# Two steps of the second phase's weight split on GpSimd, and a later place for w_k's load and split

## The chip, the cores and the metric

The kernel runs on one core of one Trainium2 chip. The metric is device time in microseconds (us), smaller is better; a time given for a kernel is the median of its runs. The engines are named as in the profile: PE is TensorE (PEld its weight loads), DVE VectorE, ACT ScalarE, POOL GpSimd, SP the queue that issues the DMAs.

## What is computed

Three stages in a row, in float32: an attention between the tokens and a small state, a gated convolution layer ("first phase" of the kernel, with the attention), and a channel mix ("second phase"). Cut to what matters:

```python
# x: (8, 8, 512, 64)  state: (8, 8, 32, 64)
a = softmax(scale * x @ state.T);  xread = a @ state          # 512 rows a head
a2 = softmax(scale * state @ x.T); sread = a2 @ x             # 32 rows a head
x1 = concat([xread, sread])            # (8, 544, 512), heads side by side

h = relu(x1 @ w_in)                    # 512 -> 1024
c = conv over 3 neighbouring tokens of h, one weight per channel and tap
x2 = (h * sigmoid(c)) @ w_out          # 1024 -> 512

xk = mu_k * x2 + (1 - mu_k) * prev(x2);  xr = mu_r * x2 + (1 - mu_r) * prev(x2)
k = relu(xk @ w_k);  v = (k * k) @ w_v;  r = sigmoid(xr @ w_r)
out = r * v                            # (8, 544, 512)
```

The weights come as float64. The kernel splits each into a high and a low float32r part, and every product of two matrices is three TensorE products: high by high, high by low, low by high.

## The kernel before

**Phases and slots.** The work is written as a row of slots. In the first phase a slot is (1, t, f): batch t (0 to 7; t = 8 holds the 32 state rows of all batches) and f, one of eight blocks of 128 of the 1024 columns. In the second it is (2, t, f), t a piece of 384 or 512 tokens. A first-phase slot has five steps: g1_main (TensorE: the block's products, lines 423 to 444), g1_a (ScalarE relu into hb, L452, ScalarE's first tap into cacc, L468, VectorE's two other taps, L470; GpSimd sets hb's two border columns, L451, and copies its last columns to carry, L453), g1_b (sigmoid on ScalarE, L478, product with hb on VectorE, L479), g1_c (the gate's high part on ScalarE, L485, its low part on VectorE, L487, or on GpSimd for t up to 2), and g1_sec (TensorE: the gate's parts by w_out into four sums acc). For t = 8 GpSimd fills hb from carry (L456, L457). The text calls the gate of slot (1, t, f) simply (t, f). The second-phase steps are g2_main to g2_sec (L566 to 618); load_y (L525) and mix (L546) prepare its input.

**m.** For the batches after the first, attention's scores and w_in are first folded to a small matrix m per batch. pair_m (L229) makes it for two batches at a time, and each of its pieces leaves through four DMAs on SP (L248) into me0, me1 (even batch) and m_odd (odd batch). g1_main of the two batches reads those.

**The weights.** Weights.load (L131) issues the DMAs of a pair of blocks; Weights.split (L145) makes the two parts of a pair, 128 x 1024 columns at a time, in seven steps: L161 and L163 on ScalarE (the lower and the upper word of the float64), L164 on VectorE (sign), L165 on VectorE (the lower word's magnitude, clamped to a range), L166 on VectorE (joined), L168 on ScalarE (the high part), L169 on VectorE (the low part). The staging tiles raw and mid have two buffers each, which pair_m's pieces use too. In the second phase there are ten such pairs: four of w_k (tiles k0, k2, k4, k6), four of w_v (v0 twice, v4 twice), two of w_r (r0, r2). They are laid out from slot (1, 7, 2) on (L753 to 767), when the pool of attention's tiles is closed.

**What sets the order.** Each engine runs its own queue in order. The queues are made when the program is built, by a scheduler that takes instructions by a priority and by its own picture of when an operand is ready. A step's priority is 1000 times its slot number plus STAGE; weights get 500 times the half-slot in which they are needed, less 1000 (weight_at, L725). behind(i) (L174) adds an edge: what is written inside it stands behind instruction i on i's own engine.

Of the kernel before, what the change touches and what calls it, by code (L numbers as in the profile page):

```python
# [8 lines left out]
F32 = mybir.dt.float32  # L9
# [23 lines left out]
def tile_kernel(  # L33
# [38 lines left out]
    N = 512  # L72
# [47 lines left out]
    class Weights:  # L120

        def __init__(self, src, many, n, pool, tag="", home=None):
            self.src, self.many, self.n, self.pool, self.tag, self.home = src, many, n, pool, tag, home
            self.wide = src[0].dtype != F32
# [18 lines left out]
        def split(self, w, first=0):  # L145
# [6 lines left out]
            if not self.wide:  # L152
# [11 lines left out]
            nc.vector.scalar_tensor_tensor(v, e, 0x80000000, v, op0=ALU.bitwise_and, op1=ALU.bitwise_or)  # L164
            nc.vector.tensor_scalar(xf, xf, scalar1=2.0, scalar2=most, op0=ALU.max, op1=ALU.min)  # L165
            nc.vector.scalar_tensor_tensor(v, x, 3, v, op0=ALU.logical_shift_left, op1=ALU.bitwise_or)  # L166
            return (
                nc.scalar.activation(hi, vf, AF.Copy),  # L168
                nc.vector.tensor_tensor(lo, vf, hi.bitcast(F32), op=ALU.subtract),  # L169
            )  # L170
# [6 lines left out]

    def weight(src, key, tag, pool, k, many, group, home=None):


        r = Weights([src[k + i] for i in range(many)], many, N, stg, home=home)

# [46 lines left out]
    def pair_m(b, q, g):  # L229
# [16 lines left out]
        for j, rj in HALF:  # L246
            for i, ri in HALF:
                nc.sync.dma_start(out=m_of(b + j, q)[ri, :, g].bitcast(F32), in_=r[rj, :, i].bitcast(F32))  # L248

# [224 lines left out]
    def g1_b(t, f):  # L474
        n = width(t)
        s = st1[t, f]
        g = s["g"] = cp.tile([P, N], F32, tag="g", name="g")
        nc.scalar.activation(g[:, :n], s["a"][:, :n], AF.Sigmoid)  # L478
        nc.vector.tensor_tensor(g[:, :n], g[:, :n], s["hb"][:, 1:1 + n], op=ALU.mult)  # L479

# [269 lines left out]
    for i in range(len(slots) + 2):  # L750
        if i < len(slots):
            ph, t, f = slots[i]
            if (ph, t, f) == (1, B - 1, 2):  # L753
                ap_cm.__exit__(None, None, None)
                p2 = ctx.enter_context(tc.tile_pool(name="p2", bufs=1))
                for k in range(0, KF, 2):
                    w = weight(w_k, "k", "wk", p2, k, 2, 2)
                    h = h2 + 2 * k
                    weight_at(w, h, h - 4)
                for k in range(0, KF, 2):  # L760
                    w = weight(w_v, "v", "wa", wp, k, 2, 4)
                    h = h2 + 2 * k + 4
                    weight_at(w, h + 1, h - 3)
                for k in range(0, KC, 2):
                    w = weight(w_r, "r", "wb", wp, k, 2, 2)
                    h = h2 + 8
# [84 lines left out]
```

## Time and profile before

| | us |
|---|---|
| median of 3 runs | 886.2 |
| lowest, highest | 883.36, 887.11 |
| profiled execution | 881.77 |
| its span, first to last instruction | 879.9 |
| busy in it: PE, DVE, ACT, POOL | 853.5, 546.4, 545.6, 105.4 |

The profile is of one execution; its times run from the span's start. PE's busy time is 97% of the span, so what is read from the profile is where PE is not busy, or not at full clock, and which engine it waits for there. Busy shares of the other engines are means over phases that differ: VectorE is busy for 95% and more of many stretches of the first phase, and for about half of the second.

### The profile page before, as it was taken

How to read it: one execution, taken by the hardware profiler on the slowest of the kernel's cores; microseconds unless marked ns; L12 is line 12 of the kernel's file. 1: busy time of each engine (PE TensorE's matmuls, PEld its weight loads, DVE VectorE, ACT ScalarE, POOL GpSimd, SP SyncE). 2: the span in 40 equal slices, each digit the busy share in tenths (PEclk: the TensorE clock that was granted, in tenths of full speed). 3: DMA queues.
4: the chain of work that ended last, by engine and by line, in shares of the span. 5: the costliest groups of instructions: out<-in, count | busy, mean ns of one | idle time of the engine just before them, and what ended most of it. 6: DMA issues, size and time to landing. Idle time of an engine off the chain costs nothing.

```text
span 879.9 us, 11844 instructions
## 1 busy us (share of the span) xinstructions
PE 853.5 (97%) x4406; PEld 686.2 (78%) x4406; DVE 546.4 (62%) x908; ACT 545.6 (62%) x952; POOL 105.4 (12%) x215
## 2 busy tenths in 40 slices
PE   5989999999999997999999999999999999999997
PEld 2557787788778775899888888888888888888886
DVE  6899987899799879999645533425334253332311
ACT  6787875787578658888756645636356364553421
POOL 1144543422111111210000000000000000000000
PEclk7899999999999998999999999999999999999999
DMA  9351254525534364233210211011100111001010
GB/s 340 116 197 49 102 143 128 150 75 160 156 114 121 96 197 151 96 144 120 98 48 37 49 48 31 17 48 49 48 23 26 49 48 48 19 18 48 1 48 36
DMA packets 45512, 76.85 MB, mean 87 GB/s; under 512 B 8336, under 2 KB 30352, under 8 KB 43408
## 3 DMA queue, kind: packets, MB, share of 16 engines
q1 hardware_dynamic: 45456, 76.12, 26.6%
q8 instruction: 34, 0.56, 0.3%
q14 instruction: 22, 0.18, 0.1%
HBM read 45.66 MB, written 17.86 MB: 72 GB/s over the span
## 4 chain that ended last, share of the span: by engine, by line
PE 88%; DVE 5%; ACT 3%; DMA 2%; SPq 1%; issue 1%; DVEq 0%; ACTq 0%
PE acc L115 14%; PE acc L116 14%; PE acc L117 14%; PE kps L115 7%; PE kps L116 7%; PE kps L117 7%; PE rps L117 4%; PE rps L116 4%; PE rps L115 4%; PE hps L115 3%; PE hps L117 3%; PE hps L116 3%; PE p_s L297 2%; PE p_m L116 1%; PE p_m L117 1%; SPq L248 1%
## 5 line engine op out<-in xcount | busy, mean ns | idle before, releaser
L594 DVE TENSOR_TENSOR ks<-k,ks 128x512 fp32r<-128x512 f32 (+1 forms) x72 | 47.6, 662 | 119.8 <-ACT ks L593 119.2
L116 PE MATMUL kps<-xk,k 128*128 128x512 f32 (+1 forms) x288 | 110.1, 382 | 0.0
L115 PE MATMUL kps<-xk,k 128*128 128x512 f32 (+1 forms) x288 | 110.1, 383 | 0.0
L117 PE MATMUL kps<-xk,k 128*128 128x512 f32 (+1 forms) x288 | 110.0, 382 | 0.0
L116 PE MATMUL acc<-gs,out 128*128 128x512 f32 (+1 forms) x288 | 109.6, 382 | 0.0
L117 PE MATMUL acc<-gs,out 128*128 128x512 f32 (+1 forms) x288 | 109.1, 380 | 0.0
L115 PE MATMUL acc<-v,ks 128*128 128x512 f32 x272 | 106.7, 392 | 0.0
L116 PE MATMUL acc<-v,ks 128*128 128x512 f32 x272 | 105.9, 389 | 0.0
L117 PE MATMUL acc<-v,ks 128*128 128x512 f32 x272 | 105.8, 392 | 0.0
L470 DVE SCALAR_TENSOR_TENSOR cacc<-hb,vcol,cacc 128x512 f32<-128x512 f32 (+1 forms) x138 | 103.3, 759 | 3.2 <-ACT cacc L468 2.7
L115 PE MATMUL acc<-gs,out 128*128 128x512 f32 (+1 forms) x288 | 95.0, 391 | 5.8 <-ACT gs L485 5.8
L559 DVE SCALAR_TENSOR_TENSOR mix<-yt,muc,mix 128x384 f32<-128x384 f32 (+7 forms) x128 | 61.4, 500 | 47.0 <-ACT mix L557 46.2
L593 ACT ACTIVATE ks<-k 128x512 fp32r<-128x512 f32 (+1 forms) x72 | 43.5, 605 | 71.2 <-PE acc L117 71.0
L557 ACT ACTIVATE mix<-yt,om 128x384 f32<-128x384 f32 (+7 forms) x128 | 61.5, 516 | 33.0 <-DMA yt<-y 16.2
L580 ACT ACTIVATE k<-kps 128x512 f32<-128x512 f32 (+1 forms) x72 | 40.9, 569 | 50.4 <-PE kps L117 50.0
L115 PEld LDWEIGHTS acc<-gs,out 128*128 128x128 f32 x288 | 54.0, 192 | 18.3 <-ACT gs L485 7.3
L116 PEld LDWEIGHTS acc<-gs,out 128*128 128x128 f32 x288 | 54.2, 188 | 13.1 <-issue 2.5
L565 DVE TENSOR_TENSOR xr<-mix,xr 128x512 fp32r<-128x512 f32 (+1 forms) x36 | 23.8, 661 | 62.8 <-ACT xr L564 62.8
L117 PEld LDWEIGHTS acc<-gs,out 128*128 128x128 f32 x288 | 54.2, 188 | 10.6 <-issue 0.8
L116 PEld LDWEIGHTS kps<-xk,k 128*128 128x128 f32 x288 | 54.4, 189 | 10.4
L117 PEld LDWEIGHTS kps<-xk,k 128*128 128x128 f32 x288 | 54.3, 188 | 10.2
L115 PEld LDWEIGHTS kps<-xk,k 128*128 128x128 f32 x288 | 54.2, 188 | 10.2
(138 smaller groups left out, 1762.1 us busy)
## 6 DMA issues: line engine op xcount, KB each, us to landing
out<-r SPq DMA_DIRECT2D x34, 256.0 KB, 2.0
xT<-x_t SPq DMA_DIRECT2D x32, 256.0 KB, 4.0
xn<-x_n SPq DMA_DIRECT2D x8, 1024.0 KB, 4.9
y<-yo SPq DMA_DIRECT2D x8, 1024.0 KB, 4.3
me<-m SPq DMA_DIRECT2D x48, 128.0 KB, 2.4
m_odd<-m SPq DMA_DIRECT2D x48, 128.0 KB, 2.4
raw<-w_out SPq DMA_DIRECT2D x8, 512.0 KB, 4.7
raw<-w_k SPq DMA_DIRECT2D x8, 512.0 KB, 4.5
```

Source lines behind the costliest of these rows:

```text
L115: nc.tensor.matmul(ps, lh, rh, start=start and k == 0, stop=False)
L116: nc.tensor.matmul(ps, lh, rl, start=False, stop=False)
L117: nc.tensor.matmul(ps, ll, rh, start=False, stop=stop and k == last)
L248: nc.sync.dma_start(out=m_of(b + j, q)[ri, :, g].bitcast(F32), in_=r[rj, :, i].bitcast(F32))
L297: nc.tensor.matmul(self.v["s", g][NS * j:NS * (j + 1), :], sT[self.b][r, h // 2, h % 2], xT[self.b][r, h // 2], start=True, stop=True,)
L470: nc.vector.scalar_tensor_tensor(a[:, :n], hb[:, k:k + n], w[k], a[:, :n], op0=ALU.mult, op1=ALU.add)
L557: nc.scalar.activation(tmp[:, o:o + m], y[:, c, q - 1:q - 1 + m], AF.Copy, scale=om[:, i:i + 1])
L559: nc.vector.scalar_tensor_tensor(tmp[:, o:o + m], y[:, c, q:q + m], muc[:, i:i + 1], tmp[:, o:o + m], op0=ALU.mult, op1=ALU.add,)
L565: nc.vector.tensor_tensor(dst[t][:, 1, c, :n], tmp[:, :n], hi.bitcast(F32), op=ALU.subtract)
L580: nc.scalar.activation(k[:, :n], s["p"][:, :n], AF.Relu)
L593: nc.scalar.activation(ks[:, 0, :n], s["k2"][:, :n], AF.Copy)
L594: nc.vector.tensor_tensor(ks[:, 1, :n], s["k2"][:, :n], ks[:, 0, :n].bitcast(F32), op=ALU.subtract)
```

## The change

Two things. Weights takes a helper engine: for the second phase's weights that is GpSimd, which now does the clamp (L165) and the low part (L169); VectorE keeps L164 and L166. And w_k's load and split get fixed places: the load stands behind the last copy of m on SP, the split's ScalarE steps behind the sigmoid and its VectorE steps behind the gate product of slot (7, 0), that is batch 7's first gate.

```diff
--- before.py
+++ after.py
@@ -121,7 +121,8 @@
 
 
 
-        def __init__(self, src, many, n, pool, tag="", home=None):
+        def __init__(self, src, many, n, pool, tag="", home=None, helper=None):
+            self.helper = helper or nc.vector
             self.src, self.many, self.n, self.pool, self.tag, self.home = src, many, n, pool, tag, home
             self.wide = src[0].dtype != F32
 
@@ -162,11 +163,11 @@
             most = float.fromhex("0x1.dffffep+32")
             nc.scalar.activation(v, v, AF.Copy, scale=0.936 * 2.0**-29)
             nc.vector.scalar_tensor_tensor(v, e, 0x80000000, v, op0=ALU.bitwise_and, op1=ALU.bitwise_or)
-            nc.vector.tensor_scalar(xf, xf, scalar1=2.0, scalar2=most, op0=ALU.max, op1=ALU.min)
+            self.helper.tensor_scalar(xf, xf, scalar1=2.0, scalar2=most, op0=ALU.max, op1=ALU.min)
             nc.vector.scalar_tensor_tensor(v, x, 3, v, op0=ALU.logical_shift_left, op1=ALU.bitwise_or)
             return (
                 nc.scalar.activation(hi, vf, AF.Copy),
-                nc.vector.tensor_tensor(lo, vf, hi.bitcast(F32), op=ALU.subtract),
+                self.helper.tensor_tensor(lo, vf, hi.bitcast(F32), op=ALU.subtract),
             )
 
     W = {}
@@ -175,10 +176,23 @@
 
         return tc.issue_after(i.ins)
 
-    def weight(src, key, tag, pool, k, many, group, home=None):
-
-
-        r = Weights([src[k + i] for i in range(many)], many, N, stg, home=home)
+    marks = {}
+
+    def after(fn, *keys):
+
+
+        def run():
+            with ExitStack() as stack:
+                for key in keys:
+                    stack.enter_context(behind(marks[key]))
+                fn()
+
+        return run
+
+    def weight(src, key, tag, pool, k, many, group, **how):
+
+
+        r = Weights([src[k + i] for i in range(many)], many, N, stg, **how)
 
         def split(first=0, n=many):
             g = (key, "group", k // group)
@@ -245,7 +259,9 @@
         nc.vector.tensor_tensor(r[:, 1], src, r[:, 0].bitcast(F32), op=ALU.subtract)
         for j, rj in HALF:
             for i, ri in HALF:
-                nc.sync.dma_start(out=m_of(b + j, q)[ri, :, g].bitcast(F32), in_=r[rj, :, i].bitcast(F32))
+                marks["m"] = nc.sync.dma_start(
+                    out=m_of(b + j, q)[ri, :, g].bitcast(F32), in_=r[rj, :, i].bitcast(F32)
+                )
 
     class Attention:
         def __init__(self, b, ap):
@@ -475,8 +491,8 @@
         n = width(t)
         s = st1[t, f]
         g = s["g"] = cp.tile([P, N], F32, tag="g", name="g")
-        nc.scalar.activation(g[:, :n], s["a"][:, :n], AF.Sigmoid)
-        nc.vector.tensor_tensor(g[:, :n], g[:, :n], s["hb"][:, 1:1 + n], op=ALU.mult)
+        marks["sigmoid", t, f] = nc.scalar.activation(g[:, :n], s["a"][:, :n], AF.Sigmoid)
+        marks["gate", t, f] = nc.vector.tensor_tensor(g[:, :n], g[:, :n], s["hb"][:, 1:1 + n], op=ALU.mult)
 
     def g1_c(t, f):
         n = width(t)
@@ -754,15 +770,16 @@
                 ap_cm.__exit__(None, None, None)
                 p2 = ctx.enter_context(tc.tile_pool(name="p2", bufs=1))
                 for k in range(0, KF, 2):
-                    w = weight(w_k, "k", "wk", p2, k, 2, 2)
+                    w = weight(w_k, "k", "wk", p2, k, 2, 2, helper=nc.gpsimd)
+                    w = after(w[0], "m"), after(w[1], ("sigmoid", B - 1, 0), ("gate", B - 1, 0))
                     h = h2 + 2 * k
                     weight_at(w, h, h - 4)
                 for k in range(0, KF, 2):
-                    w = weight(w_v, "v", "wa", wp, k, 2, 4)
+                    w = weight(w_v, "v", "wa", wp, k, 2, 4, helper=nc.gpsimd)
                     h = h2 + 2 * k + 4
                     weight_at(w, h + 1, h - 3)
                 for k in range(0, KC, 2):
-                    w = weight(w_r, "r", "wb", wp, k, 2, 2)
+                    w = weight(w_r, "r", "wb", wp, k, 2, 2, helper=nc.gpsimd)
                     h = h2 + 8
                     weight_at(w, h, h - 2)
                 at_half(2 * i + 4, lambda: load_y(0, p2))
```

What the scheduler makes of it, at three places. The names carry buffer numbers here, to tell like rows apart; before and after number lines differently (L161 to L169 are L162 to L170 after, L452 is L468, L468 is L484, L478 is L494, L485 is L501, L487 is L503, L456 is L472).

First, ScalarE ahead of the high part of gate (6,4), which is gs_3355; hb_3361 is the relu of (6,6), g_3321 and g_3358 the sigmoids of (6,4) and (6,5). Before:

```order
L452 ACTIVATE hb_3361<-hps_3348 128x512
L168 ACTIVATE k0_4040<-raw_4037 128x1024
L478 ACT_TABLE_LOAD
L478 ACTIVATE g_3321<-cacc_3259 128x512
L478 ACTIVATE g_3358<-cacc_3328 128x512
L468 ACTIVATE cacc_3365<-hb_3361,vcol_97 128x512
L161 ACTIVATE mid_4135<-raw_4131 128x1024
L163 ACTIVATE raw_4131<-raw_4131 128x1024
L485 ACTIVATE gs_3355<-g_3321 128x512
```

and after, from the first tap of (6,5) on:

```order
L484 ACTIVATE cacc_3328<-hb_3324,vcol_97 128x512
L494 ACT_TABLE_LOAD
L494 ACTIVATE g_3321<-cacc_3259 128x512
L468 ACTIVATE hb_3361<-hps_3348 128x512
L494 ACTIVATE g_3358<-cacc_3328 128x512
L484 ACTIVATE cacc_3365<-hb_3361,vcol_97 128x512
L501 ACTIVATE gs_3355<-g_3321 128x512
```

The weight steps L168, L161 and L163 are gone from between; the table load and the first sigmoid stand ahead of the relu. The steps on k0 and the second pair now come behind the sigmoid of (7,0).

Second, VectorE up to the low part of gate (8,3), which is gs_3979; mid and raw are the weights' staging tiles, xk0, xr0 and mix the second phase's input. Before, from behind the low part of (8,2):

```order
L165 TENSOR_SCALAR mid_4306<-mid_4306 128x1024
L470 SCALAR_TENSOR_TENSOR cacc_3944<-hb_3940,vcol_97,cacc_3944 128x286
L164 SCALAR_TENSOR_TENSOR raw_4302<-raw_4302 128x1024
L479 TENSOR_TENSOR g_3937<-g_3937,hb_3901 128x286
L565 TENSOR_TENSOR xr0_4187<-mix_4188,xr0_4187 128x384
L470 SCALAR_TENSOR_TENSOR cacc_3989<-hb_3985,vcol_97,cacc_3989 128x286
L166 SCALAR_TENSOR_TENSOR raw_4302<-mid_4306,raw_4302 128x1024
L165 TENSOR_SCALAR mid_4318<-mid_4318 128x1024
L164 SCALAR_TENSOR_TENSOR raw_4314<-raw_4314 128x1024
L470 SCALAR_TENSOR_TENSOR cacc_3989<-hb_3985,vcol_97,cacc_3989 128x286
L479 TENSOR_TENSOR g_3982<-g_3982,hb_3940 128x286
L487 TENSOR_TENSOR gs_3979<-g_3937,gs_3979 128x286
```

and after, the last twelve up to the same place:

```order
L495 TENSOR_TENSOR g_3898<-g_3898,hb_3858 128x286
L520 COPY yo_3833<-acc3_3574 128x512
L581 TENSOR_TENSOR xk0_3960<-mix_4105,xk0_3960 128x384
L495 TENSOR_TENSOR g_3937<-g_3937,hb_3901 128x286
L167 SCALAR_TENSOR_TENSOR raw_4266<-mid_4269,raw_4266 128x1024
L165 SCALAR_TENSOR_TENSOR raw_4302<-raw_4302 128x1024
L486 SCALAR_TENSOR_TENSOR cacc_3944<-hb_3940,vcol_97,cacc_3944 128x286
L503 TENSOR_TENSOR gs_3934<-g_3898,gs_3934 128x286
L575 SCALAR_TENSOR_TENSOR mix_4188<-yt_3641,muc_98,mix_4188 128x384
L486 SCALAR_TENSOR_TENSOR cacc_3944<-hb_3940,vcol_97,cacc_3944 128x286
L167 SCALAR_TENSOR_TENSOR raw_4302<-mid_4306,raw_4302 128x1024
L503 TENSOR_TENSOR gs_3979<-g_3937,gs_3979 128x286
```

The clamps L165 are gone from VectorE's queue. The second half of v0 (raw_4266), whose three VectorE steps and low part stood well ahead of this place before, is worked on here now.

Third, GpSimd where t = 8 begins: hb is filled from carry for one slot after the other. Before:

```order
L453 COPY carry_100<-hb_3735 128x2
L456 COPY hb_3774<-carry_100 128x8x2
L457 MEMSET hb_3774 128x8x2
L456 COPY hb_3813<-carry_100 128x8x2
L457 MEMSET hb_3813 128x8x2
L456 COPY hb_3858<-carry_100 128x8x2
L457 MEMSET hb_3858 128x8x2
L456 COPY hb_3901<-carry_100 128x8x2
L457 MEMSET hb_3901 128x8x2
```

and after:

```order
L469 COPY carry_100<-hb_3735 128x2
L166 TENSOR_SCALAR mid_4240<-mid_4240 128x1024
L472 COPY hb_3774<-carry_100 128x8x2
L473 MEMSET hb_3774 128x8x2
L472 COPY hb_3813<-carry_100 128x8x2
L473 MEMSET hb_3813 128x8x2
L170 TENSOR_TENSOR k4_4239<-raw_4236,k4_4239 128x1024
L472 COPY hb_3858<-carry_100 128x8x2
L473 MEMSET hb_3858 128x8x2
L170 TENSOR_TENSOR v0_4158<-raw_4155,v0_4158 128x1024
L472 COPY hb_3901<-carry_100 128x8x2
L473 MEMSET hb_3901 128x8x2
```

A clamp (L166 after) and two low parts (L170 after) stand between the fills.

On SP, the first load of w_k stood ahead of the last twelve copies of m and the second pair's behind them; now three half loads stand right behind the copies, then the first yt load, then the fourth.

## Rows read from the trace of the kernel before

**Rows 1.** Page: busy tenths of TensorE, its granted clock, in 40 slices
```profile
PE   5989999999999997999999999999999999999997
...
PEclk7899999999999998999999999999999999999999
```

**Rows 2.** Timeline, ScalarE, 328 to 336 us: start, length, engine, line, operation
```profile
328.03 0.60 ACT L452 ACTIVATE hb<-hps 128x512 f32<-128x512 f32 x1 [2.09 <-PE hps L117]
329.08 1.13 ACT L168 ACTIVATE k<-raw 128x1024 fp32r<-128x1024 f32 x1 [0.45 <-PE p_srT L396]
330.23 1.28 ACT L478 ACT_TABLE_LOAD   x1
331.52 1.15 ACT L478 ACTIVATE g<-cacc 128x512 f32<-128x512 f32 x2
332.58 0.71 ACT L468 ACTIVATE cacc<-hb,vcol 128x512 f32<-128x512 f32 x1
333.19 1.12 ACT L161 ACTIVATE mid<-raw 128x1024 f32<-128x1024 f32 x1
334.22 1.12 ACT L163 ACTIVATE raw<-raw 128x1024 uint32<-128x1024 uint32 x1
335.24 0.61 ACT L485 ACTIVATE gs<-g 128x512 fp32r<-128x512 f32 x1
```

**Rows 3.** Timeline, TensorE, 330 to 336 us; in brackets idle before, releaser
```profile
335.91 0.79 PE L115 MATMUL acc<-gs,out 128*128 128x512 f32 x1 [5.56 <-ACT gs L485]
```

**Rows 4.** Timeline, VectorE, 325 to 329 us
```profile
327.12 1.41 DVE L470 SCALAR_TENSOR_TENSOR cacc<-hb,vcol,cacc 128x512 f32<-128x512 f32 x2
```

**Rows 5.** Windows: stretch, length, busy PE, PEld, DVE, ACT, POOL; clock, DMA
```profile
335.91:340.61 4.70, 4.70 (x11) 3.73 (x12) 4.70 (x7) 4.70 (x8) 1.16 (x2) 0.50 0.01 3
```

**Rows 6.** Timeline, the queue SP that issues DMAs, 308 to 332 us
```profile
309.13 1.40 SPq L143 DMA_DIRECT2D raw<-w_k  x2
317.44 1.26 SPq L248 DMA_DIRECT2D me<-m  x2
...
326.69 0.97 SPq L143 DMA_DIRECT2D raw<-w_k  x2
```

**Rows 7.** Windows, columns as before, over the stretch summed
```profile
335.91:402.13 66.22, 66.22 (x351) 57.95 (x352) 64.94 (x101) 55.69 (x98) 12.50 (x32) 0.96 0.27 98
```

**Rows 8.** Timeline, VectorE, 395 to 402 us
```profile
395.55 0.69 DVE L165 TENSOR_SCALAR mid<-mid 128x1024 f32<-128x1024 f32 x1
...
399.40 1.22 DVE L169 TENSOR_TENSOR r<-raw,r 128x1024 fp32r<-128x1024 f32 x1
400.54 1.22 DVE L166 SCALAR_TENSOR_TENSOR raw<-mid,raw 128x1024 uint32<-128x1024 uint32 x1
401.68 0.45 DVE L487 TENSOR_TENSOR gs<-g,gs 128x286 fp32r<-128x286 f32 x1
```

**Rows 9.** Timeline, TensorE, 405 to 406 us
```profile
405.57 0.29 PE L116 MATMUL acc<-gs,out 128*128 128x272 f32 x1
```

**Rows 10.** Groups, ScalarE, 335.91 to 400.05 us: busy, mean, idle before, releaser
```profile
L485 ACT ACTIVATE gs<-g 128x512 fp32r<-128x512 f32 x11 | 6.9, 625 | 4.2 <-DVE g L479 4.2
```

**Rows 11.** Timeline, GpSimd and VectorE, 78 to 82 us
```profile
79.26 1.67 POOL L487 TENSOR_TENSOR gs<-g,gs 128x512 fp32r<-128x512 f32 x1 [0.52 <-ACT gs L485]
...
78.44 0.74 DVE L470 SCALAR_TENSOR_TENSOR cacc<-hb,vcol,cacc 128x512 f32<-128x512 f32 x1
...
79.70 1.78 DVE L470 SCALAR_TENSOR_TENSOR cacc<-hb,vcol,cacc 128x512 f32<-128x512 f32 x1
```

**Rows 12.** Timeline, GpSimd, operations that stand alone
```profile
1.07 0.29 POOL masks.py:199 TENSOR_SCALAR_AFFINE_SELECT ident<-ident 128x128 f32<-128x128 f32 x1
...
1.38 1.80 POOL L652 MEMSET aux<- 128x2048 f32 x1
...
88.81 1.29 POOL L487 TENSOR_TENSOR gs<-g,gs 128x512 fp32r<-128x512 f32 x1 [0.65 <-ACT gs L485]
...
181.65 0.74 POOL L227 TENSOR_TENSOR aux<-sT,aux 128x256 fp32r<-128x256 f32 x1 [2.66 <-ACT aux L226]
```

## The prediction

> **What bounds the kernel now.** I read the page's 40 slices first: TensorE is busy in nearly all of them at full clock, and one slice in the middle, 330 to 352 us, falls to 7 tenths with its clock at 8 [rows 1]. That slice is where the change acts. The waits of TensorE there say why: the first product with gate (6,4) (batch 6, column block 4) starts at 335.91 after 5.56 us of waiting for ScalarE to write the gate's high part [rows 3]. ScalarE's own timeline shows what stood ahead of it: the high part of w_k's first pair (L168, 1.13), the sigmoid's table (1.28), the two sigmoids, then the first two steps of w_k's second pair (L161 and L163, 1.12 each) [rows 2]. The wait also costs clock: from 335.91 to 340.61 TensorE works at 0.50 [rows 5], the lower of its two levels, so 4.70 us of work yield 2.35.
>
> From there to 405.57 TensorE has no gap, but VectorE is nearly as tight: it is busy 64.94 of the 66.22 us that end at 402.13 with the low part of gate (8,4) [rows 7, 8], which TensorE takes up 3.4 us later [rows 9]. In that time ScalarE waits 4.2 us for VectorE's gate products [rows 10]. So VectorE is a second bound just behind TensorE, and the change hands work to an engine that shares something with it.
>
> **Part 1, the stall.** In the changed order the first and second w_k pairs leave ScalarE's queue ahead of gate (6,4). I redo the chain from the same rows. High (6,4) now needs: relu of (6,6), which waits for TensorE and so stays at 328.03, ending 0.6 later at 328.6; sigmoid (6,5), 0.6, for which VectorE has one tap pass left after 327.2 [rows 4], to 329.2; first tap of (6,6), 0.7, to 329.9; high part, 0.6, to 330.5 [rows 2]. The table load moves ahead of the relu, into the 2.09 us in which ScalarE waits for TensorE. TensorE would arrive at 335.91 - 5.56 = 330.35, so 0.15 of the wait is left: gain 5.41. The clock fell during that wait of 5.56 us; with 0.15 of it left I take the clock to stay at 1.0: gain 2.35. Together 7.76. TensorE's waits for the copies of m around 324 and 327 stay: no time.
>
> **Part 2, the loads.** On SP, w_k's first load stood ahead of twelve m copies, yet SP was through with it at 310.5 and idle until 317.44, when VectorE released m [rows 6]; taking it away gains nothing. It now issues after the last copy, about 326.7 where the second pair's load stands today [rows 6], and ScalarE first reads it behind the sigmoid of (7,0), some 12 us later; that distance covers it. Behind it on SP the first yt load waits for two more half-pair loads; its reader, the first mix, is 15 instructions further on ScalarE. If that cover failed, mix would hold ScalarE by about 2 us once. No time for either.
>
> **Part 3, GpSimd.** Of ten weight pairs VectorE loses ten clamps L165 and ten subtractions L169. It gets back, per pair, 0.6 (0.69 less the 0.08 by which neighbours overlap) and 1.14 (399.40 to 400.54) [rows 8]. What GpSimd needs is bounded by its own operations [rows 12]. The subtraction: a two-input operation takes 0.74 at 256 columns and 1.29 at 512, so at 1024 an estimated 1.29 + 2 x 0.55 = 2.39. The clamp has no row. Below: a memset only writes, 1.80 for 2048, so 0.9. Above: the subtraction, 2.39. The nearest row reads one tile and writes one, the identity's mask, 0.29 for 128 columns, which less 0.1 of start makes 1.6; it also works out a mask, so I take 1.3, between memset and mask.
>
> What makes this dear is that the two engines hold each other up. GpSimd's L487 at 79.26 lets VectorE's running product end, then VectorE's next tap takes 1.78 where the same tap takes 0.74 [rows 11]: held 1.04 by an operation that alone takes 1.29 [rows 12]. So a hold is GpSimd's time less about 0.25: 2.15 per subtraction, 1.05 per clamp (0.65 to 2.15 by its bounds). In this stretch almost every VectorE operation reads two tiles of SBUF, as that tap does, and VectorE is without idle time in which a hold could pass unseen.
>
> The Trainium skill ("SBUF — State Buffer", section "SBUF: two separate sides") says that the port pair is locked for the whole instruction and the loser waits for all of it. The row shows 1.04 of 1.29. By the page the sum below would end at 892.9 instead of 890.0.
>
> **The sum.** I take the stretch from TensorE's restart to its first use of the low part of (8,4). TensorE's time for it is now 405.57 - 335.91 = 69.66, less 2.35 of clock = 67.3; the changed order puts five 512-column products fewer (0.23 each) ahead of that use: 66.1. VectorE's queue in the same stretch: 64.94, less five clamps and five subtractions (3.0 and 5.7), plus what the order moves into it (one 512- and one 286-column tap, less one 286-column product, plus a small subtraction: 0.9) = 57.1. It keeps today's idle time, 66.22 - 64.94 = 1.3: 58.4. So far VectorE is 7.7 ahead: the offload would do its work. Now the holds: up to (8,4) GpSimd has six clamps and six subtractions, because w_k's first pairs, done today during the stall, now fall into this stretch: 6 x (1.05 + 2.15) = 19.2. Total 77.6, and TensorE is late by 77.6 - 66.1 = 11.5. At (8,3) the same count, with five subtractions, gives 11. After that VectorE has ever more slack (its busy share falls once the convolutions end), so nothing is added, and TensorE, busy to the end, gets nothing back. The delay comes in pieces of one to two us over ten gates; the clock's fall of today followed a wait of 5.56, so I add none.
>
> ScalarE does the same weight steps as before and about three more of them in the stretch: 55.69 + 3.1 [rows 7] of 66.1, no bound. GpSimd's border memsets and carry copies now stand behind clamps and subtractions; ScalarE's relus wait for those memsets, but each memset waits for a gate product of VectorE's first, which is later still. No time; up to 2.4 once where that cover fails.
>
> Net: -7.76 + 11.5 = +3.7. The profiled execution took 881.77 (span 879.9, 1.9 around it), so 885.5 on its scale; the runs' median is 886.2, so **890.0**, 0.4% slower. About 0.5% is what a measurement of this kernel can tell from no change.
>
> **The rivals.**
> 1. *The holds don't bite.* If GpSimd's work fell into moments when VectorE does not need the shared path, VectorE would be 7.7 ahead and only the gain stays: 886.2 - 7.8 = 878.4. For it: 58.4 against 66.1. Against it: 1.3 us of idle time for 19 of holds.
> 2. *Only the subtractions hold.* The clamp has one input, and no row shows a one-input operation of size on GpSimd beside VectorE. Then 58.4 + 12.9 - 66.1 = 5.2 late, net -2.6: 883.6.
> 3. *Slower: the clamp is as dear as the subtraction.* Its hold is then 2.15: 58.4 + 25.8 - 66.1 = 18.1 late, net +10.3: 896.5. It decides from a hold of 1.17, that is a clamp of 1.42 us, where the loss passes 0.5%; pauses as long as today's, with the clock at half again, would come on top, some 2 us each.
>
> The Trainium skill ("GPSIMD Engine Reference", section "Elementwise — side-by-side cycle accounting") gives a body of up to two operations 1.03 cycles per element; at 1.2 GHz an estimated 0.9 us for the clamp, the lower bound above, and the sum would be 887.6. No run here shows it yet.
>
> That the change doesn't do what it says is no rival: in the built order w_k's first ScalarE step stands behind sigmoid (7,0), and ten clamps and ten subtractions stand on GpSimd.
>
> **How the numbers follow.** Forecast 0.50 (887 to 894, by clamps of 0.8 to 2.0 us), rival 1 0.22, rival 2 0.10, rival 3 0.18. Of the forecast, 0.20 lies over 890.6 and 0.30 below; rival 2 splits 0.03 faster, 0.07 same. Faster 0.25, same 0.37, slower 0.38. The range runs from rival 1 to rival 3: 878 to 897.
>
> **What would show it.** TensorE's first product with (6,4) at about 330.5, and clock 1.0 through 330 to 345: part 1 right. GpSimd's L165 and L169 near 1.3 and 2.4 and VectorE's two-input operations beside them 1 to 2 us longer: part 3 right. TensorE waiting some 11 us for VectorE's gate parts between 343 and 405: the sum right. VectorE idle more than 5 us in that stretch with TensorE gapless means rival 1. I am wrong if GpSimd's operations overlap VectorE's without lengthening them, or if another wait takes the stall's place at 330.

## The result: 0.65% slower, and where the time went

| | before | after |
|---|---|---|
| median of 11 runs, us | 884.38 | 890.7 |
| lowest, highest | 881.85, 891.34 | 888.03, 893.03 |
| ratio of times over all runs, 95% interval | | 1.0065 (1.0044 to 1.0085) |
| profiled execution, its span | 881.77, 879.9 | 889.33, 887.4 |

The forecast was 890.0 on a base of 886.2, a ratio of 1.0043. The page of the changed kernel, against [rows 1]: the dip of TensorE's busy share and clock near 340 us is gone; a lower share stands at 377 to 399 instead, where VectorE is full; GpSimd is no longer idle there.

```profile
span 887.4 us, 11864 instructions
...
PE   5989999999999999989999999999999999999997
...
DVE  6999987799799879999664443425334253332221
...
POOL 1134543322111115775700000000000000000000
PEclk8899999999999999999999999999999999999999
```

**The stall is gone, as forecast.** ScalarE's timeline, the answer to [rows 2], and under it TensorE's (in brackets idle before, and who ended it):

```profile
327.04 1.28 ACT L494 ACT_TABLE_LOAD   x1
328.33 0.63 ACT L494 ACTIVATE g<-cacc 128x512 f32<-128x512 f32 x1
329.85 0.60 ACT L468 ACTIVATE hb<-hps 128x512 f32<-128x512 f32 x1 [0.88 <-PE hps L117]
330.34 0.62 ACT L494 ACTIVATE g<-cacc 128x512 f32<-128x512 f32 x1
330.86 0.71 ACT L484 ACTIVATE cacc<-hb,vcol 128x512 f32<-128x512 f32 x1
331.47 0.62 ACT L501 ACTIVATE gs<-g 128x512 fp32r<-128x512 f32 x1
...
332.15 1.20 PE L115 MATMUL acc<-gs,out 128*128 128x512 f32 x4
...
391.04 0.40 PE L115 MATMUL acc<-gs,out 128*128 128x272 f32 x1 [2.45 <-DVE yo L520]
...
423.55 0.50 PE L117 MATMUL rps<-r,xr 128*128 128x512 f32 x1 [0.36 <-DVE xr L581]
...
435.04 0.44 PE L115 MATMUL kps<-xk,k 128*128 128x384 f32 x1 [1.05 <-ACT k L596]
...
446.02 0.50 PE L115 MATMUL kps<-xk,k 128*128 128x512 f32 x1 [1.40 <-ACT xk L580]
```

The first product with gate (6,4) starts at 332.15 without a wait, where before it waited 5.56 [rows 3]. The windows (length, busy PE, PEld, DVE, ACT, POOL, then clock) show full clock behind it, where [rows 5] had 0.50, and in 345 to 405 a VectorE that is busy 59.71 of 60:

```profile
330.00:345.00 15.00, 15.00 (x66) 11.68 (x65) 14.18 (x22) 13.97 (x23) 6.25 (x11) 1.00 0.50 188
345.00:405.00 60.00, 54.79 (x294) 46.15 (x293) 59.71 (x73) 45.61 (x80) 41.23 (x37) 0.97 0.34 123
390.00:398.00 8.00, 6.96 (x43) 6.96 (x44) 8.00 (x12) 7.97 (x16) 7.50 (x7) 0.79 0.33 133
```

**Time lost, gate by gate.** One execution differs from the next by a few us already ahead of the change (waits for copies of m near 163 us, 1.81 in this profile and none in that of before, and in some other profiles the clock behind them: this one is 2.2 us behind that of before at gate (6,3)). So I compare from there on. For one product, found in both traces by its place in the kernel's order, I take its start less the columns of all products queued ahead of it (0.21 us for 512 at full clock); the difference to before is the time lost. The gain is read at gate (6,5), the loss up to gate (8,4), and what comes later up to 456 us. All kernels of this study, us:

| kernel | gain at (6,5) | loss to (8,4) | later | net | ratio of times (95%) |
|---|---|---|---|---|---|
| the changed kernel | -8.1 | 9.7 | 3.7 | +5.3 | 1.0065 (1.0044 to 1.0085) |
| e1: placement alone | -7.9 | 7.7 | -0.1 | -0.3 | 0.9999 (0.9984 to 1.0014) |
| e2: helper alone | -1.4 | 8.1 | 3.8 | +10.6 | 1.0121 (1.0102 to 1.0141) |
| e3: placement, clamp on GpSimd | -8.0 | 8.8 | -0.1 | +0.6 | 1.0004 (0.9988 to 1.0020) |
| e4: placement, low part on GpSimd | -8.0 | 12.8 | 1.6 | +6.4 | 1.0065 (1.0042 to 1.0087) |
| e13: changed kernel, copy for low part | -8.3 | 4.7 | -0.1 | -3.8 | 0.9958 (0.9944 to 0.9971) |
| e5: split behind (6,4) | -6.9 | 9.3 | 0.0 | +2.4 | 1.0008 (0.9996 to 1.0020) |
| e9: only the load moved | -8.3 | 11.3 | 1.4 | +4.4 | 1.0050 (1.0032 to 1.0068) |
| e10: two steps held back | -5.1 | 9.0 | -0.1 | +3.8 | 1.0048 (1.0031 to 1.0064) |
| e11: placement, w_v later | -7.8 | 4.7 | -0.2 | -3.4 | 0.9964 (0.9947 to 0.9981) |
| e12: split behind (6,4), w_v later | -6.9 | 10.4 | -0.2 | +3.3 | 1.0038 (1.0019 to 1.0057) |

The net is read from one trace each, the ratio from all runs against runs of the kernel before in the same session; the two agree within about 2 us.

**GpSimd and VectorE side by side.** The timeline of both, in three places:

```profile
345.03 3.75 POOL L166 TENSOR_SCALAR mid<-mid 128x1024 f32<-128x1024 f32 x1
...
355.11 2.90 POOL L170 TENSOR_TENSOR k<-raw,k 128x1024 fp32r<-128x1024 f32 x1 [0.98 <-ACT k L169]
...
381.31 2.78 POOL L170 TENSOR_TENSOR v<-raw,v 128x1024 fp32r<-128x1024 f32 x1
...
345.21 1.53 DVE L503 TENSOR_TENSOR gs<-g,gs 128x512 fp32r<-128x512 f32 x1
346.66 1.21 DVE L167 SCALAR_TENSOR_TENSOR raw<-mid,raw 128x1024 uint32<-128x1024 uint32 x1
...
355.65 2.93 DVE L495 TENSOR_TENSOR g<-g,hb 128x512 f32<-128x512 f32 x1
...
381.70 2.70 DVE L486 SCALAR_TENSOR_TENSOR cacc<-hb,vcol,cacc 128x286 f32<-128x286 f32 x1
...
384.92 0.50 DVE L486 SCALAR_TENSOR_TENSOR cacc<-hb,vcol,cacc 128x286 f32<-128x286 f32 x1
```

A low part (2.4 to 2.9) holds VectorE for 1.6 to 2.2: the gate product at 355.65 takes 2.93 instead of 0.69, the tap at 381.70 takes 2.70, and the same tap alone, at 384.92, 0.50. A clamp takes 3.6 to 4.2, yet holds VectorE only once, by 0.5 to 0.85: the operation at 345.21 takes 1.53 instead of 0.68, and the join behind it, two inputs too, runs at its usual 1.21 while the clamp goes on for two more us. Summed over VectorE's operations up to the low part of (8,4), what they take beyond their usual length is 17.0 us; behind it 8.1 more.

### The profile page after: what moved, and what is told of

It reads as the page before. It is cut to its first block, busy times and chain, and to the rows that moved or that the text cites. A ratio compares the mean times of both kernels' runs of the same rounds, so it can differ in the third digit from the quotient of the medians.

```text
span 887.4 us, 11864 instructions
## 1 busy us (share of the span) xinstructions
PE 857.3 (97%) x4406; PEld 685.2 (77%) x4406; DVE 553.3 (62%) x888; ACT 545.1 (61%) x952; POOL 165.2 (19%) x235
## 4 chain that ended last, share of the span: by engine, by line
PE 76%; DVE 13%; ACT 4%; DMA 3%; issue 2%; SPq 1%; POOL 1%; DVEq 0%; ACTq 0%; POOLq 0%
PE acc L115 12%; PE acc L116 12%; PE acc L117 11%; PE kps L115 7%; PE kps L116 6%; PE kps L117 6%; PE rps L117 3%; PE rps L116 3%; PE rps L115 3%; DVE cacc L486 3%; PE hps L115 2%; PE hps L117 2%; PE hps L116 2%; PE p_s L313 2%; DVE raw L167 2%
## 5 line engine op out<-in xcount | busy, mean ns | idle before, releaser
L610 DVE TENSOR_TENSOR ks<-k,ks 128x512 fp32r<-128x512 f32 (+1 forms) x72 | 49.8, 692 | 118.8 <-ACT ks L609 118.3
L486 DVE SCALAR_TENSOR_TENSOR cacc<-hb,vcol,cacc 128x512 f32<-128x512 f32 (+1 forms) x138 | 113.5, 832 | 3.3 <-ACT cacc L484 2.7
L575 DVE SCALAR_TENSOR_TENSOR mix<-yt,muc,mix 128x384 f32<-128x384 f32 (+7 forms) x128 | 64.6, 526 | 48.8 <-ACT mix L573 48.0
```

The costliest lines, as they stand in the source:

```text
L486: nc.vector.scalar_tensor_tensor(a[:, :n], hb[:, k:k + n], w[k], a[:, :n], op0=ALU.mult, op1=ALU.add)
L575: nc.vector.scalar_tensor_tensor(tmp[:, o:o + m], y[:, c, q:q + m], muc[:, i:i + 1], tmp[:, o:o + m], op0=ALU.mult, op1=ALU.add,)
L610: nc.vector.tensor_tensor(ks[:, 1, :n], s["k2"][:, :n], ks[:, 0, :n].bitcast(F32), op=ALU.subtract)
```

## The experiments

**e1, e2: the change's two halves.** e1 leaves the helper out:

```diff
-                    w = weight(w_k, "k", "wk", p2, k, 2, 2, helper=nc.gpsimd)
+                    w = weight(w_k, "k", "wk", p2, k, 2, 2)
```
(the same for w_v and w_r). 

> The changed kernel with only the new places of w_k's load and split; clamp (L166) and low part (L170) go back to VectorE. Theory (the loss is GpSimd holding VectorE up): no holds, so VectorE needs, up to the low part of gate (8,4), the 58.4 us of the prediction plus six clamps at 0.6 and six low parts at 1.14, 68.8 against TensorE's 66.1: 2.7 late, against a gain of 8.1 at gate (6,4). Expected 884.4 - 5.4 = 879.0, ratio 0.992 to 0.996, TensorE without a wait for gate (6,4) and with under 4 us of waits between 343 and 450. Rival (the later place alone crowds the weights into VectorE's tight stretch, the helper is harmless): 887 or more, with TensorE's waits between 343 and 450 near the 10 us of the changed kernel.

e2 leaves the placement out:

```diff
-                    w = after(w[0], "m"), after(w[1], ("sigmoid", B - 1, 0), ("gate", B - 1, 0))
```


> The changed kernel with only the helper: clamp and low part on GpSimd for all ten pairs, but w_k's load and split where the kernel before has them. Theory: the stall at gate (6,4) stays (w_k's steps stand ahead of it on ScalarE again), at 5 us or more, with the clock at 0.5 behind it; holds of 0.8 per clamp and 2.2 per low part for five pairs, 15.0, less the 8.7 that VectorE is spared, against its 3.4 us of lead: 2.8 late by (8,4), and up to 4 more behind it as in the changed kernel. Expected 887 to 892, ratio 1.003 to 1.008. Rival (the placement makes the loss): 884 or less.

Measured: e1 0.9999, no change; e2 1.0121. Neither half is good. e2 was worse than expected: it keeps the stall (TensorE still waits 5.0 for gate (6,4)) and pays for the helper, 6.7 us up to (8,4) where I had 2.8. Most of these come at one place: a wait of 3.25 at 397.84, and a granted clock of 0.50 from there to 403.4. e1 was expected at 0.992 to 0.996 and misses that: the gain of 7.9 is there, and a loss of 7.7 takes it back without a single held operation. So the loss is not the helper's alone: beside the placement the helper costs 0.66%, some 5.8 us. The halves do not simply add up. Without the placement the same helper costs 1.21%, 10.7 us; so the placement is worth some 5 us beside the helper and nothing without it.

Where e1 loses: its VectorE needs 73.6 us from TensorE's first product with (6,4), 334.27, to the low part of (8,4), 407.89, where I had 68.8. The list of its operations there against those of the kernel before tells why: beside the clamps and low parts that I had counted, 3.3 us more stand ahead of (8,4) in this order than in the changed one (the sign, clamp and join of r2's pair, one more gate product and one more xr, less a tap). The other 1.6 my list for the changed kernel lacked as well: there 76.0 less 17.0 of holds is 59.0, almost without idle time, where I had 57.1 of work. VectorE's idle time in e1, 1.2, is about what I had. TensorE's longest loss there is a new wait, here in ScalarE's and TensorE's timeline of e1:

```profile
393.15 1.15 ACT L162 ACTIVATE mid<-raw 128x1024 f32<-128x1024 f32 x1 [2.43 <-DMA raw<-w_r]
...
397.04 0.44 ACT L501 ACTIVATE gs<-g 128x286 fp32r<-128x286 f32 x1 [0.22 <-DVE g L495]
...
397.53 0.79 PE L115 MATMUL acc<-gs,out 128*128 128x272 f32 x4 [3.15 <-ACT gs L501]
```

ScalarE stands at the first step of w_r, which waits for its load; SP issued that load at 387.86, as soon as v0's low part on VectorE (386.62, 1.22 long) had freed one of the two staging buffers. The gates behind it in ScalarE's queue wait too, and TensorE 3.15 with them.

**e3, e4: the helper's two steps.** Each puts one back on VectorE:

```diff
-                self.helper.tensor_tensor(lo, vf, hi.bitcast(F32), op=ALU.subtract),
+                nc.vector.tensor_tensor(lo, vf, hi.bitcast(F32), op=ALU.subtract),
```


> The changed kernel with the low part (L170) back on VectorE, the clamp (L166) still on GpSimd. Theory: the clamp takes 3.7 us on GpSimd but holds VectorE for only some 0.8, so VectorE needs 58.4 + 6 x 1.14 + 6 x 0.8 = 70.0 up to (8,4): 3.9 late, net -4.2, expected 880, ratio 0.993 to 0.997. Rival (the clamp's 3.7 us is what makes TensorE late, because VectorE's joining step L167 and ScalarE's high part wait for it): close to the changed kernel, 887 to 891.

```diff
-            self.helper.tensor_scalar(xf, xf, scalar1=2.0, scalar2=most, op0=ALU.max, op1=ALU.min)
+            nc.vector.tensor_scalar(xf, xf, scalar1=2.0, scalar2=most, op0=ALU.max, op1=ALU.min)
```


> The changed kernel with the clamp (L166) back on VectorE, the low part (L170) still on GpSimd. Theory: the low part holds VectorE for 2.2 us each time, so 58.4 + 6 x 0.6 + 6 x 2.2 = 75.2 up to (8,4): 9.1 late, and up to 4 more behind it; net +1 to +5, expected 888, ratio 1.001 to 1.006. Rival (the clamp's length makes the loss): near 880, ratio 0.995.

Measured: e3 1.0004, the same as the placement alone; e4 1.0065, the same as the whole change. The clamp on GpSimd costs nothing and brings nothing, 3.7 us long as it is: a hold of up to 0.85 is about the 0.6 that VectorE is spared. e3's trace has VectorE busy for 70.6 us up to (8,4), 1.9 less than e1's, but idle for 4.6 instead of 1.2, mostly waiting for ScalarE, so nothing comes of it. All of the helper's loss is the low part's. (e4 lies just above the range that I expected, e3 0.3% and e1 0.4% above theirs.)

**e13: is it the hold, or the longer way of a weight pair through the queues?** The changed kernel with another operation in the low part's place:

```diff
-                self.helper.tensor_tensor(lo, vf, hi.bitcast(F32), op=ALU.subtract),
+                (nc.gpsimd.tensor_copy(lo, vf) if self.helper is nc.gpsimd
+                 else nc.vector.tensor_tensor(lo, vf, hi.bitcast(F32), op=ALU.subtract)),
```


> The changed kernel with the subtraction of the low part (L170) replaced by a copy on GpSimd, of the same 128x1024 elements with one input instead of two (so the second phase's weights have a wrong low part; the subtraction is left out). GpSimd stays as full of operations, in nearly the same order, but in the probe such a copy took 1.46 and held VectorE for 0.9, where the subtraction took 2.4 to 2.8 and held it for 2.2. Theory (the holds are the helper's cost): 6 x 1.3 = 7.8 less of holds up to (8,4) and 5 us less behind it, so TensorE is 2 late instead of 10 and has no new waits behind 410: 883, ratio 0.995 to 1.000. Rival (the order of the queues, with GpSimd's steps between the weights' steps, is the helper's cost): 888 to 891 as the changed kernel.

Measured: 0.9958, 9 to 10 us less than the changed kernel, by one operation that still runs on GpSimd. (The kernel leaves the subtraction out, so this is a time to learn from and not one to have.) GpSimd's groups in it (count, busy, mean ns) show that the clamps are as long as ever and that a copy takes about half of a subtraction; under them TensorE's waits from 343 to 450 (total, times, longest), down to one kind:

```profile
L166 POOL TENSOR_SCALAR mid<-mid 128x1024 f32<-128x1024 f32 x10 | 38.0, 3802 | 13.7 <-ACT mid L162 13.7
...
L171 POOL CAST k<-raw 128x1024 fp32r<-128x1024 f32 x4 | 6.0, 1505 | 5.7 <-DVE raw L167 5.7
```
```profile
PE acc L115 <- ACT gs L505: 3.0, 2, 2.3
```

The holds up to (8,4) fall from 17.0 to 8.3, VectorE's time from 76.0 to 69.2, TensorE's loss from 9.7 to 4.7, and nothing is lost later. Part of that is work that is truly left out (a copy has one input less to read), but VectorE has the same list to do, and the clamps, with the detour through GpSimd's queue, are still there; so the detour by itself costs little. That the hold is what costs is then what VectorE's timeline shows. A copy is also 1.2 us shorter than the subtraction and so frees its staging buffer earlier; e13 does not separate this from the shorter hold.

**e7: what the clamp is.** GpSimd operations of seven forms, each twice, in the second phase of the kernel before, beside additions of two SBUF tiles on VectorE (two stands for max and min):

```diff
+                forms = [
+                    lambda: nc.gpsimd.tensor_scalar(a, a, scalar1=2.0, scalar2=8.0, **two),
+                    lambda: nc.gpsimd.tensor_scalar(a, a, scalar1=2.0, scalar2=None, op0=ALU.max),
+                    lambda: nc.gpsimd.tensor_scalar(a[:, 0], a[:, 0], scalar1=2.0, scalar2=8.0, **two),
+                    lambda: nc.gpsimd.tensor_scalar(a, a, scalar1=1.0, scalar2=0.0, op0=ALU.mult, op1=ALU.add),
+                    lambda: nc.gpsimd.tensor_copy(a, r[:, :, :, 0]),
+                    lambda: nc.gpsimd.tensor_tensor(a, r[:, :, :, 0], a, op=ALU.subtract),
+                    lambda: nc.gpsimd.tensor_tensor(a, a, d, op=ALU.subtract),
+                ]
```


> The kernel before, with GpSimd operations on tiles of no use added in the second phase, where GpSimd has nothing to do, and 49 additions of two SBUF tiles (128x512) on VectorE beside them; the output is the reference's, the total time is of no interest. The forms: clamp as in the changed kernel (two operations, 128x1024), one of its two operations alone, the clamp at 512 columns, multiply and add in its place, a copy from every second word, the subtraction as in the changed kernel, the subtraction of two contiguous tiles. Theory: the clamp takes 3.6 as in the changed kernel because each of its two operations passes over the tile, so one alone takes 1.8 to 2.0, and 512 columns take 1.8; it holds VectorE's additions by no more than 0.8, while both subtractions (2.4) hold them by 2. Rival (max and min are what is dear): multiply and add take 1.3 or less, and one max alone still over 2.5.

GpSimd's timeline, then VectorE's:

```profile
432.38 3.63 POOL L781 TENSOR_SCALAR pa<-pa 128x1024 f32<-128x1024 f32 x1
438.27 3.26 POOL L782 TENSOR_SCALAR pa<-pa 128x1024 f32<-128x1024 f32 x1 [2.27 <-DVE pa L791]
...
446.64 1.98 POOL L783 TENSOR_SCALAR pa<-pa 128x512 f32<-128x512 f32 x1 [0.59 <-DVE pa L791]
...
452.65 1.31 POOL L784 TENSOR_SCALAR pa<-pa 128x1024 f32<-128x1024 f32 x1 [0.84 <-DVE pa L791]
...
458.29 1.41 POOL L785 COPY pa<-pr 128x1024 f32<-128x1024 f32 x1 [1.52 <-DVE pa L791]
...
474.83 2.82 POOL L786 TENSOR_TENSOR pa<-pr,pa 128x1024 f32<-128x1024 f32 x1 [1.87 <-DVE pa L791]
...
438.81 1.52 DVE L565 TENSOR_TENSOR xk<-mix,xk 128x512 fp32r<-128x512 f32 x1
...
446.76 1.09 DVE L793 TENSOR_TENSOR pd<-pd 128x512 f32<-128x512 f32 x1
...
475.37 2.82 DVE L793 TENSOR_TENSOR pd<-pd 128x512 f32<-128x512 f32 x1
```

The rival is right for the length: multiply and add, two operations as well, take 1.31 over the same tile; one max alone takes 3.26, nearly the clamp's 3.63. So it is the max that is dear on GpSimd, not the second operation (a min alone was not run). The hold does not follow the length: 0.84 by the max at 438 (1.52 for 0.68), 0.41 by the clamp of 512 columns, 2.14 by the subtraction.

**e5, e9, e10: could the stall go for less?** Without a helper, the first w_k pairs at other places. e5 puts the split behind the high part of (6,4) (the mark "high" is that step of g1_c) and leaves the load alone:

```diff
-                    w = after(w[0], "m"), after(w[1], ("sigmoid", B - 1, 0), ("gate", B - 1, 0))
+                    w = w[0], after(w[1], ("high", B - 2, 4))
```


> All on VectorE, w_k's load where the scheduler puts it (ahead of the last copies of m), w_k's split behind the high part of gate (6,4) instead of behind batch 7's first gate: only the stall is avoided, nothing is held back beyond it. Theory (VectorE is a second bound: what the stall used to hide, it must do in the stretch up to (8,4), wherever the weights stand in it): VectorE has the same 72 us of work there as with the placement alone, against TensorE's 66; only its 1.7 us of idle time can go. Expected net 0 to -2, ratio 0.997 to 1.000, TensorE's waits spread over 345 to 405. Rival (the placement alone is no gain because the late loads make ScalarE wait 7 us for raw in two staging buffers): that wait falls below 3 us, TensorE waits under 3 us in 345 to 405, and the time is 880, ratio 0.994.

e9 moves only the load:

```diff
+                    w = after(w[0], "m"), w[1]
```


> All on VectorE, only the load of w_k has its new place (behind the last copy of m); the split has no edge. In this order, too, no weight step stands ahead of gate (6,4) on ScalarE, and w_k's first steps come some 6 us earlier than with both edges. Theory (VectorE as second bound): gain of 8 at gate (6,4), loss of 6 to 8 up to (8,4), ratio 0.997 to 1.001. Rival (the split's late place is what costs): 881, ratio 0.995.

e10 holds back two steps alone, the high part of the first pair (late is the mark behind which it stands) and the second pair's split:

```diff
+            with behind(marks[late]) if late else ExitStack():
+                high = nc.scalar.activation(hi, vf, AF.Copy)
...
+                    if k == 2:
+                        w = w[0], after(w[1], ("high", B - 2, 4))
```


> All on VectorE, loads where the scheduler puts them; only two steps are held back behind the high part of gate (6,4): the high part of w_k's first pair (L169 here) and the start of the second pair. The first pair's sign, clamp and join on VectorE (2.9 us) stay ahead of 330, where VectorE has idle time. Theory: VectorE's work behind 330.5 is then that of the kernel before, 71.8 us from 330.35 to 402.13, against TensorE's 66 to 67: 5 late, against a gain of 8. Expected net -3, 882.5, ratio 0.995 to 0.998: better than both kernels, and the low part of (8,4) on VectorE ends where it does before. Rival (ScalarE, not VectorE, is what the stretch waits for): no better than the placement alone, ratio 1.000.

Measured: 1.0008, 1.0050, 1.0048, all three above the ranges that I expected. The theory of a sum over the whole stretch was wrong for e9 and e10. Each has its gain at (6,4), and each loses more than that in one later stall with the clock behind it. TensorE's and ScalarE's timelines, of e5, e9 and e10 in turn:

```profile
345.50 0.50 PE L116 MATMUL acc<-gs,out 128*128 128x512 f32 x1 [1.74 <-DVE gs L503]
351.34 2.08 PE L115 MATMUL acc<-gs,out 128*128 128x512 f32 x4 [3.72 <-ACT gs L501]
```
```profile
364.00 2.08 PE L115 MATMUL acc<-gs,out 128*128 128x512 f32 x4 [4.77 <-ACT gs L501]
...
361.25 1.16 ACT L162 ACTIVATE mid<-raw 128x1024 f32<-128x1024 f32 x1 [2.91 <-DMA raw<-w_k]
```
```profile
347.51 2.08 PE L115 MATMUL acc<-gs,out 128*128 128x512 f32 x4 [3.67 <-ACT gs L503]
...
343.73 1.14 ACT L162 ACTIVATE mid<-raw 128x1024 f32<-128x1024 f32 x1 [2.03 <-DMA raw<-w_v]
```

The four products behind each wait of 3.67 and more take 2.08 where four take 1.20 at full clock: such a wait costs clock again. In e9 and e10 ScalarE waits in order for a load that SP could issue only when a low part on VectorE had freed a staging buffer, and the next gates stand behind it; in e5 it is mostly VectorE, which has no idle time from 334 to 350 and has 8 us of weights ahead of the gates (6,6) and (6,7). Right behind (6,4) TensorE is one or two gates behind the other engines, so steps for the weights there cost about their length: those 8 us of e5, where the table has 9.3 of loss. Of the four places, those of e1 (behind batch 7's first gate, as in the change) and e5 cannot be told apart, and the other two are worse. A third staging buffer wasn't tried, so how much of e9's and e10's loss it would save is open.

**e11, e12: less VectorE work in the stretch.** v0, split ahead of (8,4) in all kernels so far, is first read near 424. e11 is e1 with another order of the pairs:

```diff
-                    weight_at(w, h, h - 4)
+                    weight_at(w, h, h2 + 1 if k == 4 else h - 4)
...
-                    weight_at(w, h + 1, h - 3)
+                    weight_at(w, h + 1, h - 1 if k == 0 else h - 3)
...
-                    weight_at(w, h, h - 2)
+                    weight_at(w, h, h2 + 2)
```


> Placement alone (all on VectorE, as in e1), and the four w_v blocks that are split first come later: the pairs are worked on in the order k0, k2, k4, r0, r2, v0, v0, k6, v4, v4 instead of k0, k2, v0, k4, v0, r0, r2, k6, v4, v4. In the built order both v0 pairs and the low part of r0 then stand behind the low part of gate (8,4) on VectorE; together they are 4.3 + 4.3 + 1.1 = 9.7 us of its work. Theory (VectorE's work up to (8,4) is the bound: 73.6 us with the placement alone against TensorE's 66.1): it falls to about 64 to 66, the gain of 8 at gate (6,4) stays for the most part, and what is late later (v0 is first read at about 424) costs under 3. Expected 880, ratio 0.992 to 0.997. Rival (ScalarE waiting in order for the weights' loads is the bound; its steps only change places): 884 or more, ratio 0.999 to 1.004.

e12 is e11 with e5's place for the split. 

> As e11_late_v, but with w_k's load where the scheduler puts it and w_k's split behind the high part of gate (6,4) instead of behind batch 7's first gate (the place of e5). Theory: the same work for VectorE up to (8,4), but 8.6 us of it directly behind gate (6,4), where TensorE is only one or two gates behind: a wait of 3 to 5 there as in e5, that is not given back. Expected 883, ratio 0.995 to 1.000. Rival (only the sum up to (8,4) counts): the same time as e11_late_v within 0.2%.

Measured: e11 0.9964, 881.9 us against 885.35: faster than both kernels. VectorE needs 64.6 up to the low part of (8,4), as expected (9.0 less than in e1), the loss falls from e1's 7.7 to 4.7, and nothing is lost later, though VectorE now does v0 behind 405. What is left of TensorE's waits there in e11 (in total, times, longest):

```profile
PE acc L115 <- ACT gs L501: 2.6, 2, 1.3
...
PE acc L115 <- ACT yo L522: 0.8, 1, 0.8
```

e12 has the same work for VectorE (busy 64.8 us up to there, e11 64.0), and 1.0038, above the range that I expected: the stall of e5 is there again.

```profile
351.41 2.08 PE L115 MATMUL acc<-gs,out 128*128 128x512 f32 x4 [3.28 <-ACT gs L501]
```

So the sum of VectorE's work up to (8,4) counts, as e1 and e11 show, but it does not decide alone: in e12 weight steps stand where TensorE has no lead to give, and even e11, whose 64.6 are below TensorE's 66.1, loses 4.7, of which the waits above are 3.4 and the rest is not traced.

## Why the prediction came out right, step by step

**What bounds the kernel**, a stall at (6,4) and VectorE as a second bound just behind TensorE: right. It is the main result: with the stall gone, the placement alone (e1) gains nothing; with 9.0 us of VectorE's time taken out of the stretch (e11) it gains 0.36%.

**Part 1, the stall:** forecast 7.76 with clock, measured 8.1. The high part of (6,4) was forecast to end at 330.5; it ends at 332.09 in a trace that is 2.2 behind: 329.9.

**Part 2, the loads at no time:** right for w_k's own load, which was all that I looked at. The chain of loads behind it (two staging buffers, freed by the low part) is what makes ScalarE wait, 3.15 us of TensorE in e1 and 4.77 in e9. The changed kernel pays for it once, later (with VectorE's and GpSimd's rows, in order of time):

```profile
419.55 3.48 DVE L167 SCALAR_TENSOR_TENSOR raw<-mid,raw 128x1024 uint32<-128x1024 uint32 x1
...
423.06 1.15 ACT L169 ACTIVATE k<-raw 128x1024 fp32r<-128x1024 f32 x1 [2.11 <-DVE raw L167]
...
424.28 2.44 POOL L170 TENSOR_TENSOR k<-raw,k 128x1024 fp32r<-128x1024 f32 x1 [2.34 <-ACT k L169]
...
426.75 0.80 SPq L144 DMA_DIRECT2D raw<-w_v  x2
...
432.44 1.17 ACT L162 ACTIVATE mid<-raw 128x1024 f32<-128x1024 f32 x1 [2.35 <-DMA raw<-w_v]
...
434.52 0.46 ACT L596 ACTIVATE k<-kps 128x384 f32<-128x384 f32 x1
...
438.23 5.77 POOL L170 TENSOR_TENSOR v<-raw,v 128x1024 fp32r<-128x1024 f32 x2 [0.83 <-ACT v L169]
...
441.61 2.80 DVE L610 TENSOR_TENSOR ks<-k,ks 128x384 fp32r<-128x384 f32 x1
```

**Part 3, GpSimd:** the subtraction, forecast 2.39 with a hold of 2.15, measured 2.4 to 2.9 with 2.2: right. The clamp, forecast 1.3 between 0.9 and 2.39, took 3.6 to 4.2 (37.9 us for ten): outside both bounds. The bounds came from operations that write, select or subtract; none of them was a max, and e7 shows that 1.31 is what a multiply and add would have taken. The hold that I derived from it (length less 0.25, 1.05) came out near the measured 0.8 by luck: two errors met, a length too short by 2.4 and a rule that does not hold for the clamp. By my own rule a clamp of 3.7 would have held 3.4.

The Trainium skill ("SBUF — State Buffer", section "SBUF: two separate sides") has the loser wait for the whole instruction. For the subtraction the trace comes near that (2.2 of 2.4 to 2.9); for the clamp it disagrees (0.8 of 3.7), and the measurement decides. The 1.03 cycles per element of the Trainium skill ("GPSIMD Engine Reference", section "Elementwise — side-by-side cycle accounting"), an estimated 0.9 us, do not hold for max and min: 3.6.

**The sum:** VectorE's time to the low part of (8,4) was forecast at 77.6, measured 76.0 (332.15 to 408.11); TensorE late by 11.5, measured 9.7; holds 19.2, measured 17.0 (six low parts at about 2.1, six clamps at some 0.75). Right within 2 us or a little over.

**The step that failed** is "After that VectorE has ever more slack, so nothing is added": 3.7 us more were lost behind (8,4). The rows above are most of the causes. At 419.55 and 441.61 VectorE's join and the low part of k squared are held by 2.3 each by low parts of the weights on GpSimd, and what follows makes TensorE wait 0.36 and 1.40. The join that is held leads to one wait more: the pair's high part on ScalarE waits 2.11 for it and its low part on GpSimd starts at 424.28; when this ends, at 426.72, it frees a staging buffer and SP issues the next load of w_v; the first step of that pair on ScalarE waits 2.35 for it at 432.44, and behind it in the queue stands the relu at 434.52, for which TensorE waits 1.05. VectorE's busy share is a mean; in the second phase its operations and ScalarE's wait for each other one by one, and a hold of 2.2 in such a chain is not covered by idle time elsewhere. e13, where the holds behind (8,4) add up to 3.5 instead of 8.1, loses nothing there.

**Clock:** I added none for the new waits. The longest, 2.45 at 391.04, was followed by a clock of 0.79 over 390 to 398, which is 1.7 us. That is part of the 9.7.

**The rivals:** "the holds don't bite" and "only the subtractions hold" fall with the two timelines side by side: the holds are there, and a clamp holds some 0.8. The slower rival had the clamp as dear as the subtraction, with the same hold. It is dearer, but holds far less, so the rival's time (896.5) did not come. That the clamp costs nothing net is e3's result.

**What I could not have said from the sum:** it gave the helper 19.2 - 10.4 = 8.8 and the placement 2.7 of loss. Measured up to (8,4), the helper adds 2.0 to the placement's loss of 7.7 (9.7 in all), and its other 3.8 come behind (8,4). The sum for the stretch was near because the two misses have opposite signs, and that is luck: in the changed order fewer of the weights' steps stand ahead of (8,4) than in e1's, and my sum, made for the changed order, could not be split. The net, +3.7 against +5.3, is near for the same sort of reason: too much loss up to (8,4), 1.8, and none behind it, where 3.7 came.

## What to carry to other kernels

When a stall goes, the next bound is the engine that used the stall to catch up: add up its work to the first product that needs it, and move work that is needed later out of that stretch, before handing work to a helper. A helper that shares a path with the engine to be relieved is paid by its hold, not by its length: here one with one input held some 0.8 to save 0.6 and was a wash, one with two inputs held up to 2.2 to save 1.1. Where a step waits for a load, look at what stands behind it in its own queue, and at who frees the buffer that the load needs.

## What the runs showed of the hardware

- GpSimd's max and min in fp32 took 3.63 us for 128 x 1024 (one max alone 3.26), where multiply and add took 1.31 and a copy from every second word 1.41 (e7).
- GpSimd's hold of a VectorE operation with two SBUF inputs was 0.4 for one input of 512 columns, 0.8 to 0.9 for one of 1024, whether the GpSimd operation took 1.3 or 3.7, and 1.4 to 2.2 for two inputs of 1024 columns (e7; in the changed kernel the clamps, 1024 columns, held 0.5 to 0.85).
- TensorE's clock stayed full behind waits of 1.94 (e10, gate (6,4)) and 3.15 (e1, 397.53), but fell behind one of 2.45 in the changed kernel, and within or behind those of 3.7 to 4.8 in e5, e9 and e10. The length of one wait alone does not tell.
